# Weight decoding in a chained attention and expert kernel: GpSimd takes the signs and 26 low halves, VectorE joins a step after ScalarE's copy

## The chip, the cores and the metric

The kernel runs on one core of a Trainium2 chip. A core has a matrix engine (TensorE, PE in the profile; its weight loads are PEld), a vector engine (VectorE, DVE), a scalar engine (ScalarE, ACT), GpSimd (POOL) and SyncE (SP), which issues most of the transfers. The metric is the device time of one execution in microseconds (us), the median of several runs. Lower is better.

## The reference

Three stages follow each other, each in float32:

```python
# q, k, v: (2, 6016, 256)
qn = q / (norm(q, axis=1) + 1e-6); kn = k / (norm(k, axis=1) + 1e-6)
a = softmax(kn.transpose(0, 2, 1) @ qn / tau)           # (2, 256, 256)
x = (v @ a).reshape(12032, 256)
h = x @ w_in                                            # (12032, 2048)
x = (h - tanh(h)) @ w_out                               # (12032, 256)
return (sigmoid(x @ w_gate) * (x @ w_val)) @ w_out2     # 1536 hidden columns
```

The weights `w_in`, `w_out`, `w_gate`, `w_val` and `w_out2` arrive as float64, so each of their elements is two 32-bit words. They are the operands that this change is about.

## The kernel before, in words

**Blocks and steps.** The 12032 tokens are cut into 24 blocks of 496 or 512 columns (`blocks`, 12 for each of the two batches). The attention matrix of a batch is multiplied into `w_in` once (`aw_chunk`), so that a block needs only `H` = (A w_in) v (`emit_H`, L332 and L334), the activation (`emit_E`, L342 to L350), the product with `w_out` (`emit_X`, L373 in block 0, L378 to L381 later), and then gate, value and output (`emit_GV`, `emit_S`, `emit_O`). One turn of the main loop is a step `T`: it issues H of one of the 16 hidden tiles f of a block, the activation of the tile before it, X of the one before that, and what `gv_at` puts there of the gate stage. Block 0 has the steps 0 to 15, block 1 the steps 16 to 31. The program is written in the order in which each engine runs it: every engine, and SP's queue of transfers, takes its instructions strictly in that order and waits for semaphores where an operand is not there.

**Nearly float32 products.** Most matrix products split each operand into a rounded high half and a low half (operand minus high half) and add three products. The high half is a ScalarE copy, the low half a subtraction on VectorE.

**Weights on the way in.** `conv` turns a piece of float64 weights into float32. There are 34 pieces of 512 KB: 8 of `w_in` (`conv_win`), 8 of `w_out` (`conv_w1`), 18 of the gate stage (`conv_m2`). For each piece: a transfer into a staging tile `st` (L125); ScalarE scales the high words into `cb` (L135) and writes an f16 of them beside the mantissa bits (L136); VectorE shifts 16-bit halves (L138) and joins (L143). A piece of the gate stage then gets its high half on ScalarE (L149) and its low half on VectorE (L150). For `w_out` the halves come later, in `split_w1` (L184, L187).

**What sets the order.** `conv` is a generator. Wrapped in `whole`, it runs from one bare `yield` to the next in one step (`yield 1` does not end a step there). `at(T, ...)` starts it: its transfer is issued at the end of step T, the rest at the end of the following steps, after the activation of that step in the order of ScalarE and VectorE. The pieces of `w_out` with i > 1 start at step 2i - 1, those of the gate stage where the loop over `n` puts them.

**Buffers.** The staging tiles of `w_out` and of the gate stage come from the pool `v4`, which has 3 buffers and also holds the `v` tiles. From step 4 to step 16 one of the three holds `v` of block 1. The pieces of `w_out` then follow each other in one buffer, those of the gate stage in the other. A transfer into a buffer waits until the last reader of the piece before it is done.

Of the kernel before, what the change touches and what calls it, by code (L numbers as in the profile page):

```python
# [8 lines left out]
F32 = mybir.dt.float32  # L9
F32R = mybir.dt.float32r  # L10
BF16 = mybir.dt.bfloat16
U32 = mybir.dt.uint32
U16 = mybir.dt.uint16
F16 = mybir.dt.float16
AF = mybir.ActivationFunctionType
ALU = mybir.AluOpType
AX = mybir.AxisListType
# [10 lines left out]
def kernel(  # L28
# [13 lines left out]
    nc = tc.nc  # L42
# [18 lines left out]
    rest, i = N - WB * nb, nb // 2  # L61
    assert 0 <= rest <= nb * (TB - WB)
    while rest:
        widths[i] += QB
        rest -= QB
        i = (i + 1) % nb
    blocks = []
    for b in range(B):
        t = 0
# [23 lines left out]
    def cv(name, shape=(P, 512)):  # L93
        return cv_p.tile(list(shape), F32, tag="cv", name=name)
# [22 lines left out]
    w1_hi = [wp.tile([P, 2, C], F32R, name=f"w1h{i}") for i in range(N1 // 2)]  # L117
    w1_lo = {}
    win_d = dr_p.tile([N1 // 2, P, NK, 2 * P], F32, name="win_d")

    def conv(src, shape, pool, tag, name, w=None, hi=None, lo=None):

        a, m = shape
        st = pool.tile([P, a, 2 * m], U32, tag=tag, name=f"st_{name}")
        nc.sync.dma_start(out=st, in_=src)  # L125
        yield
        words = st.rearrange("p a (m t) -> p a m t", t=2)
        low, high = words[:, :, :, 0], words[:, :, :, 1]
        half = st.bitcast(U16).rearrange("p a (m t) -> p a m t", t=4)
        bt = cv(f"cb_{name}", (P, a, m))  # L130
        bu = bt.bitcast(U32)

        nc.scalar.activation(bt, high.bitcast(F32), AF.Copy, scale=2.0**-112)  # L135
        nc.scalar.activation(half[:, :, :, 3].bitcast(F16), high.bitcast(F32), AF.Copy, scale=2.0**-96)  # L136
        yield 1
        nc.vector.tensor_scalar(half[:, :, :, 2], half[:, :, :, 1], 13, None, ALU.logical_shift_right)  # L138
        yield 1
        yield 1  # L140
        if callable(w):
            w = w()
        nc.vector.scalar_tensor_tensor(  # L143
            out=bu if w is None else w.bitcast(U32), in0=bu, scalar=3, in1=high,
            op0=ALU.logical_shift_left, op1=ALU.bitwise_or
        )
        if w is None:
            yield
            nc.scalar.activation(hi, bt, AF.Copy)  # L149
            nc.vector.tensor_tensor(out=lo, in0=bt, in1=hi.bitcast(F32), op=ALU.subtract)  # L150

    def whole(g):

        for x in g:
            if x is None:
                yield

    def words(ap):
        return ap.bitcast(U32)

    def conv_win(i, pool, tag="st"):
        src = words(w_in)[:, i * 512:(i + 1) * 512].rearrange("(k p) f -> p k f", p=P)
        yield from conv(src, (NK, 2 * P), pool, tag, f"wi{i}", w=win[i])
# [7 lines left out]
    w1_f = {}  # L171

    def conv_w1(i):
        src = words(w_out)[i * 256:(i + 1) * 256, :].rearrange("(a p) d -> p a d", p=P)

        def home():
            pool, tag = (wp, f"w1l{i - 4}") if i > 3 else (wp2, f"w2{'hl'[i % 2]}{4 + i // 2}")
            w1_f[i] = pool.tile([P, 2, C], F32, tag=tag, name=f"w1f{i}")
            return w1_f[i]

        return conv(src, (2, C), v4_p, "v4", f"w1{i}", w=home)

    def split_w1(i):
        nc.scalar.activation(w1_hi[i], w1_f[i], AF.Copy)  # L184
        yield
        w1_lo[i] = wp.tile([P, 2, C], F32R, tag=f"w1l{i}", name=f"w1l{i}")
        nc.vector.tensor_tensor(out=w1_lo[i], in0=w1_f[i], in1=w1_hi[i].bitcast(F32), op=ALU.subtract)  # L187


    kq = {}  # L190
# [291 lines left out]
    while len(e_of) < NT:  # L482
        for home in ("x2h", "x2l", *(f"rr{i}" for i in range(6))):
            j = len(e_of)
            n = min(2 if home[0] == "x" else 1, NT - j)
# [174 lines left out]
    def conv_m2(i, which):  # L660
        if which == 2:
            src = words(w_out2)[i * 256:(i + 1) * 256, :].rearrange("(a p) d -> p a d", p=P)
            for x, nm in ((w2_hi, "w2h"), (w2_lo, "w2l")):
                x[i] = wp2.tile([P, 2, 2 * P], F32R, tag=f"{nm}{i}", name=f"{nm}{i}")
            h, lo = w2_hi[i], w2_lo[i]
        else:
            w = (w_gate, w_val)[which]
            src = words(w)[:, i * 512:(i + 1) * 512].rearrange("(k p) f -> p k f", p=P)
            h, lo = ((wg_hi[i], wg_lo[i]), (wv_hi[i], wv_lo[i]))[which]
        return conv(src, (2, 2 * P), v4_p, "v4", f"m{which}{i}", hi=h, lo=lo)  # L670
# [31 lines left out]
    def at(step, fn, *a):  # L702
        bg.setdefault(step, []).append((fn, a))
# [3 lines left out]
    GV0 = (20, 21, 22, 24, 25, 27, 28, 30, 31, 33, 34, 35)  # L707
# [6 lines left out]
    for i in range(N1 // 2):  # L714
        at({6: 16, 2: 18, 7: 19, 3: 20, 4: 21, 5: 23, 0: 25, 1: 26}[i], split_w1, i)
# [4 lines left out]
            at(2 * i - 9 if i < 6 else 2 * i - 5, win_store, i)  # L720
    for n in range(3 * N2 // 2):
        i, w = divmod(n, 3)
        late = GV0[2 * i] - 3 + (w == 2)
        at(min(late, 4 + 2 * n if n < 6 else 7 + 3 * n // 2), lambda i=i, w=w: whole(conv_m2(i, w)))
    at(2 * N1 + 7, ks_load)
    for j in range(NT):
        t = 54 + 2 * j
# [121 lines left out]
```

## Time and profile before

| | us |
|---|---|
| median of 3 runs | 2211.52 (2211.27 to 2211.89) |
| profiled execution, its own time | 2212.01 |
| its span in the profile | 2210.2 |
| TensorE busy | 2199.5 |
| VectorE busy | 1772.7 |
| ScalarE busy | 1602.0 |
| GpSimd busy | 66.5 |

The span runs from the first to the last instruction of the program; the execution's own time has 1.8 us around it. A matmul's recorded time overlaps with the next one's, so a busy TensorE says that it had work, not how fast it went. The granted clock of TensorE is 1.00 in all slices. GpSimd's 46 additions (L688) lie between 366 and 858 us, and all 34 pieces of weights between 2 and 246 us.

### The profile page before, as it was taken

What the parts mean: (1) busy time and instruction counts of PE and PEld (TensorE: products, weight loads), DVE (VectorE), ACT (ScalarE), POOL (GpSimd) and SP (SyncE); (2) the same over time, 40 slices, a digit from 0 to 9 for tenths busy, and PEclk for the clock granted to TensorE, in tenths of its full rate; (3) what the DMA queues carried; (4) which work ended last, traced back from release to release, by engine and by line L of the source; (5) the groups of instructions that cost most, each with busy time, mean ns of one, the idle gap of its engine ahead of it and who ended that gap; (6) DMA issues with size and microseconds to landing.
All of it is one profiled execution on the core that took longest, in us unless ns stands there. A gap on an engine that the chain in (4) does not pass through costs nothing.

```text
span 2210.2 us, 28820 instructions
## 1 busy us (share of the span) xinstructions
PE 2199.5 (100%) x10338; PEld 1944.1 (88%) x10338; DVE 1772.7 (80%) x2723; ACT 1602.0 (72%) x2811; POOL 66.5 (3%) x53
## 2 busy tenths in 40 slices
PE   9999999999999999999999999999999999999999
PEld 8778899898888888888999999999988888888898
DVE  7889877888888888878787787787787877877773
ACT  7988867777777777767677676776776776767763
POOL 0000000111111110000000000000000000000000
PEclk9999999999999999999999999999999999999999
DMA  9742101111111010001000000000000000000000
GB/s 354 241 147 96 38 1 53 34 29 52 35 29 48 27 36 20 1 24 34 19 19 1 19 19 1 19 19 1 19 20 1 19 20 1 20 1 19 10 1 19
DMA packets 54000, 86.54 MB, mean 39 GB/s; under 512 B 4960, under 2 KB 31072, under 8 KB 53856
## 3 DMA queue, kind: packets, MB, share of 16 engines
q1 hardware_dynamic: 53280, 83.91, 11.6%
q8 instruction: 81, 1.33, 0.3%
q10 hardware_dynamic: 576, 0.79, 0.1%
q14 instruction: 63, 0.52, 0.1%
HBM read 69.73 MB, written 14.94 MB: 38 GB/s over the span
## 4 chain that ended last, share of the span: by engine, by line
PE 93%; DVE 3%; ACT 3%; issue 1%; DMA 1%; ACTq 0%; DVEq 0%
PE o L445 16%; PE h L332 14%; PE h L334 7%; PE x L381 7%; PE x L378 7%; PE x L379 7%; PE va L414 5%; PE va L416 5%; PE va L413 5%; PE ga L414 5%; PE ga L413 5%; PE ga L416 5%; PE x L373 2%; PE kqe L517 1%; PE aw L285 1%
## 5 line engine op out<-in xcount | busy, mean ns | idle before, releaser
L347 DVE SCALAR_TENSOR_TENSOR w<-u,h 128x496 f32<-128x496 f32 (+1 forms) x384 | 259.6, 676 | 228.6 <-ACT t L343 227.7
L350 DVE COPY_PREDICATED w<-m,t 128x496 f32<-128x496 uint16 (+1 forms) x384 | 303.9, 792 | 39.9 <-ACT sr L687 0.5
L342 ACT ACTIVATE u<-h 128x496 f32<-128x496 f32 (+1 forms) x384 | 222.7, 580 | 138.8 <-PE h L334 138.3
L345 ACT ACTIVATE s<-u,cb 128x496 f32<-128x496 f32 (+1 forms) x384 | 273.8, 713 | 0.3 <-DVE w L349 0.3
L346 ACT ACTIVATE m<-u,ct 128x496 bf16<-128x496 f32 (+1 forms) x384 | 272.5, 710 | 0.0
L348 DVE TENSOR_TENSOR t<-h,t 128x496 f32<-128x496 f32 (+1 forms) x384 | 258.4, 673 | 0.0
L349 DVE SCALAR_TENSOR_TENSOR w<-s,w 128x496 f32<-128x496 f32 (+1 forms) x384 | 257.6, 671 | 0.0
L332 PE MATMUL h<-vTh,awh 128*128 128x496 f32 (+1 forms) x768 | 232.8, 385 | 0.0
L334 PE MATMUL h<-vTh,awl 128*128 128x496 f32 (+1 forms) x768 | 225.1, 375 | 0.2 <-DVE awl L291 0.2
L332 PE MATMUL h<-vTl,awh 128*128 128x496 f32 (+1 forms) x768 | 225.0, 375 | 0.0
L343 ACT ACTIVATE t<-h 128x496 f32<-128x496 f32 (+1 forms) x384 | 223.1, 581 | 0.0
L414 PE MATMUL va<-x2h,wvl 128*128 128x496 f32 (+1 forms) x552 | 206.9, 375 | 0.0
L414 PE MATMUL ga<-x2h,wgl 128*128 128x496 f32 (+1 forms) x552 | 206.9, 375 | 0.0
L413 PE MATMUL va<-x2h,wvh 128*128 128x496 f32 (+1 forms) x552 | 206.9, 375 | 0.0
L413 PE MATMUL ga<-x2h,wgh 128*128 128x496 f32 (+1 forms) x552 | 206.8, 375 | 0.0
L425 DVE TENSOR_TENSOR sg<-va,sg 128x496 f32<-128x496 f32 (+1 forms) x288 | 192.2, 667 | 18.1 <-PE va L416 18.1
L424 ACT ACTIVATE sg<-ga 128x496 f32<-128x496 f32 (+1 forms) x288 | 168.6, 585 | 11.2 <-PE ga L416 11.1
L416 PE MATMUL ga<-x2l,wgh 128*128 128x496 f32 (+1 forms) x576 | 168.8, 375 | 0.0
L416 PE MATMUL va<-x2l,wvh 128*128 128x496 f32 (+1 forms) x576 | 168.8, 375 | 0.0
L332 PEld LDWEIGHTS h<-vTh,awh 128*128 128x128 f32 x768 | 144.4, 189 | 24.5 <-issue 6.8
L334 PEld LDWEIGHTS h<-vTh,awl 128*128 128x128 f32 x768 | 145.1, 189 | 17.7 <-DVE awl L291 0.6
L332 PEld LDWEIGHTS h<-vTl,awh 128*128 128x128 f32 x768 | 145.1, 189 | 17.2
(358 smaller groups left out, 4425.8 us busy)
## 6 DMA issues: line engine op xcount, KB each, us to landing
v<-in_v_dram SPq DMA_DIRECT2D x16, 496.0 KB, 4.2
out_dram<-ob SPq DMA_DIRECT2D x15, 496.0 KB, 3.0
sr<-in_q_dram SPq DMA_DIRECT2D x47, 128.0 KB, 2.1
sr<-in_k_dram SPq DMA_DIRECT2D x47, 128.0 KB, 2.3
raw<-in_q_dram SPq DMA_DIRECT2D x13, 384.0 KB, 8.1
raw<-in_k_dram SPq DMA_DIRECT2D x12, 384.0 KB, 8.2
st_wi<-in_moe_w_in_dram SPq DMA_DIRECT2D x8, 512.0 KB, 7.0
st_w<-in_moe_w_out_dram SPq DMA_DIRECT2D x8, 512.0 KB, 4.7
```

The lines of the kernel that those rows point to most:

```text
L332: MM(o[:, :n], aw_hi[i][:, kk, fs], turned(p, x[:, kk, :n]), start=x is h and kk == 0, stop=False)
L334: MM(o[:, :n], aw_lo[i][:, kk, fs], turned(p, h[:, kk, :n]), start=False, stop=kk == 1)
L345: nc.scalar.activation(s, u, AF.Square, bias=cb)
L346: nc.scalar.activation(m, u, AF.Relu, bias=ct2)
L347: nc.vector.scalar_tensor_tensor(out=w, in0=u, scalar=C2, in1=hp, op0=ALU.mult, op1=ALU.mult)
L348: nc.vector.tensor_tensor(out=t, in0=hp, in1=t, op=ALU.subtract)
L349: nc.vector.scalar_tensor_tensor(out=w, in0=s, scalar=CG, in1=w, op0=ALU.add, op1=ALU.mult)
L350: nc.vector.copy_predicated(w, m.bitcast(U16), t)
L413: MM(o[:, :n], wht[m // 2][:, d, ms], h[d], start=d == 0, stop=False)
L414: MM(o[:, :n], wlt[m // 2][:, d, ms], h[d], start=False, stop=False)
L416: MM(o[:, :n], wht[m // 2][:, d, ms], lo[d], start=False, stop=d == 1)
L445: MM(ops[p][d][:, :n], w[i][:, a, ds[d]], x, start=m == 0 and w is w2_hi and x is ph, stop=m == N2 - 1 and x is pl)
```

## The change

`conv` no longer writes the f16 on ScalarE (L136) and no longer shifts halves on VectorE (L138). GpSimd instead overwrites the high words with their sign bits, in the same step as ScalarE's copy and after it. A step later VectorE shifts the low words by 29 and joins the signs to them, in place, and then joins the result with the copy. The bare `yield` between GpSimd and VectorE is the step. The subtraction for the low half moves to GpSimd for the 18 pieces of the gate stage and for the 8 of `split_w1`. The pieces of the gate stage start one step earlier; those of `w_out` start where they did.

```diff
--- before.py
+++ after.py
@@ -11,7 +11,7 @@
 BF16 = mybir.dt.bfloat16
 U32 = mybir.dt.uint32
 U16 = mybir.dt.uint16
-F16 = mybir.dt.float16
+I32 = mybir.dt.int32
 AF = mybir.ActivationFunctionType
 ALU = mybir.AluOpType
 AX = mybir.AxisListType
@@ -126,28 +126,28 @@
         yield
         words = st.rearrange("p a (m t) -> p a m t", t=2)
         low, high = words[:, :, :, 0], words[:, :, :, 1]
-        half = st.bitcast(U16).rearrange("p a (m t) -> p a m t", t=4)
         bt = cv(f"cb_{name}", (P, a, m))
         bu = bt.bitcast(U32)
 
 
-
         nc.scalar.activation(bt, high.bitcast(F32), AF.Copy, scale=2.0**-112)
-        nc.scalar.activation(half[:, :, :, 3].bitcast(F16), high.bitcast(F32), AF.Copy, scale=2.0**-96)
+        nc.gpsimd.tensor_scalar(high.bitcast(I32), high.bitcast(F32), 0.0, -2.0**31, ALU.is_lt, ALU.mult)
         yield 1
-        nc.vector.tensor_scalar(half[:, :, :, 2], half[:, :, :, 1], 13, None, ALU.logical_shift_right)
-        yield 1
+        yield
+        nc.vector.scalar_tensor_tensor(
+            out=low, in0=low, scalar=29, in1=high, op0=ALU.logical_shift_right, op1=ALU.bitwise_or
+        )
         yield 1
         if callable(w):
             w = w()
         nc.vector.scalar_tensor_tensor(
-            out=bu if w is None else w.bitcast(U32), in0=bu, scalar=3, in1=high,
+            out=bu if w is None else w.bitcast(U32), in0=bu, scalar=3, in1=low,
             op0=ALU.logical_shift_left, op1=ALU.bitwise_or
         )
         if w is None:
             yield
             nc.scalar.activation(hi, bt, AF.Copy)
-            nc.vector.tensor_tensor(out=lo, in0=bt, in1=hi.bitcast(F32), op=ALU.subtract)
+            nc.gpsimd.tensor_tensor(out=lo, in0=bt, in1=hi.bitcast(F32), op=ALU.subtract)
 
     def whole(g):
 
@@ -184,7 +184,7 @@
         nc.scalar.activation(w1_hi[i], w1_f[i], AF.Copy)
         yield
         w1_lo[i] = wp.tile([P, 2, C], F32R, tag=f"w1l{i}", name=f"w1l{i}")
-        nc.vector.tensor_tensor(out=w1_lo[i], in0=w1_f[i], in1=w1_hi[i].bitcast(F32), op=ALU.subtract)
+        nc.gpsimd.tensor_tensor(out=w1_lo[i], in0=w1_f[i], in1=w1_hi[i].bitcast(F32), op=ALU.subtract)
 
 
     kq = {}
@@ -720,8 +720,8 @@
             at(2 * i - 9 if i < 6 else 2 * i - 5, win_store, i)
     for n in range(3 * N2 // 2):
         i, w = divmod(n, 3)
-        late = GV0[2 * i] - 3 + (w == 2)
-        at(min(late, 4 + 2 * n if n < 6 else 7 + 3 * n // 2), lambda i=i, w=w: whole(conv_m2(i, w)))
+        late = GV0[2 * i] - 4 + (w == 2)
+        at(min(late, 3 + 2 * n if n < 6 else 6 + 3 * n // 2), lambda i=i, w=w: whole(conv_m2(i, w)))
     at(2 * N1 + 7, ks_load)
     for j in range(NT):
         t = 54 + 2 * j
```

The order of SP's queue at steps 5 and 7 (`st_w13` is piece 3 of `w_out`, `st_m10` the first `w_val` piece, `er` are tiles of q and k). Before:

```order
L125 DMA st_w13_780<-in_moe_w_out_dram 128x2x512
L502 DMA er18_821<-in_q_dram 128x256
L502 DMA er18_821<-in_k_dram 128x256
L125 DMA st_m10_824<-in_moe2_w_val_dram 128x2x512
```

After:

```order
L125 DMA st_w13_780<-in_moe_w_out_dram 128x2x512
L125 DMA st_m10_782<-in_moe2_w_val_dram 128x2x512
L502 DMA er18_823<-in_q_dram 128x256
L502 DMA er18_823<-in_k_dram 128x256
L502 DMA er19_858<-in_q_dram 128x256
L502 DMA er19_858<-in_k_dram 128x256
L502 DMA er20_861<-in_q_dram 128x256
L502 DMA er20_861<-in_k_dram 128x256
L125 DMA st_w14_864<-in_moe_w_out_dram 128x2x512
L166 DMA win_d_124<-win6_114 128x512
L125 DMA st_m20_869<-in_moe2_w_out_dram 128x2x512
```

The two pieces that were issued a step apart are issued together, at the odd step, and the next two at the next odd step.

ScalarE at step 10 (`u`, `t`, `s`, `m` are the activation of tile 9, `cb` the copies out of the staging tiles). Before:

```order
L342 ACTIVATE u_9_954<-h_9_929 128x496
L343 ACTIVATE t_9_955<-h_9_929 128x496
L345 ACTIVATE s_9_956<-u_9_954,cb 128x496
L346 ACTIVATE m_9_958<-u_9_954,ct 128x496
L149 ACTIVATE w2h_909<-cb_m_940 128x512
L135 ACTIVATE cb_w_987<-st_w_951 128x512
L136 ACTIVATE st_w_951<-st_w_951 128x512
```

After:

```order
L342 ACTIVATE u_9_956<-h_9_929 128x496
L343 ACTIVATE t_9_957<-h_9_929 128x496
L345 ACTIVATE s_9_958<-u_9_956,cb 128x496
L346 ACTIVATE m_9_960<-u_9_956,ct 128x496
L149 ACTIVATE w2h_867<-cb_m_907 128x512
L133 ACTIVATE cb_w_989<-st_w_951 128x512
L133 ACTIVATE cb_m_992<-st_m_954 128x512
L342 ACTIVATE u_10_995<-h_10_969 128x496
```

One copy and one f16 write have become two copies, both ahead of the activation of tile 10 in step 11.

VectorE at step 9 (`w` closes the activation of tile 8, `awl` is the low half of a part of A w_in, `w1f` a decoded piece of `w_out`). Before:

```order
L350 COPY_PREDICATED w_8_916<-m_8_917,t_8_914 128x496
L291 TENSOR_TENSOR awl_926<-aw_5_887,awh_105 128x512
L138 TENSOR_SCALAR st_m_911<-st_m_911 128x512
L143 SCALAR_TENSOR_TENSOR cb_m_940<-cb_m_940,st_m_911 128x512
```

After:

```order
L350 COPY_PREDICATED w_8_916<-m_8_917,t_8_914 128x496
L291 TENSOR_TENSOR awl_926<-aw_5_891,awh_105 128x512
L137 SCALAR_TENSOR_TENSOR st_w_864<-st_w_864 128x512
L143 SCALAR_TENSOR_TENSOR w1f_941<-cb_w_904,st_w_864 128x512
L137 SCALAR_TENSOR_TENSOR st_m_869<-st_m_869 128x512
L143 SCALAR_TENSOR_TENSOR cb_m_907<-cb_m_907,st_m_869 128x512
```

Two pieces are joined here, both copied in step 8, and they are the last instructions of the odd step; in the even step nothing is joined.

## Rows read from the trace of the kernel before

**Rows 1.** The page, part 1: busy us (share of the span) x instructions, by engine.
```profile
PE 2199.5 (100%) x10338; PEld 1944.1 (88%) x10338; DVE 1772.7 (80%) x2723; ACT 1602.0 (72%) x2811; POOL 66.5 (3%) x53
```

**Rows 2.** Waits of TensorE, whole run: total us, times, longest us.
```profile
PE va L414 <- DVE wvl L150: 1.5, 1, 1.5
PE x L378 <- ACT g_14h L355: 0.6, 1, 0.6
PE rq L236 <- DVE dg L223: 0.5, 1, 0.5
PE ep L267 <- DVE s L257: 0.5, 2, 0.4
PE h L334 <- DVE awl L291: 0.2, 1, 0.2
```

**Rows 3.** Windows: stretch, length, then busy us (x instructions) of each engine, clock, DMA.
```profile
100.00:110.00 10.00, 10.00 (x41) 7.46 (x40) 8.79 (x15) 9.02 (x15) 0.00 (x0) 1.00 0.66 189
220.00:240.00 20.00, 18.22 (x83) 14.87 (x81) 19.30 (x31) 18.30 (x31) 0.00 (x0) 1.00 0.12 41
```

**Rows 4.** Groups by line, 0 to 420 us: shape, xcount | busy us, mean ns | idle.
```profile
L136 ACT ACTIVATE st_m<-st_m 128x512 f16<-128x512 f32 x18 | 24.5, 1363 | 0.6
L138 DVE TENSOR_SCALAR st_m<-st_m 128x512 uint16<-128x512 uint16 x18 | 13.5, 748 | 2.4 <-ACT st_m L136 2.4
L135 ACT ACTIVATE cb_m<-st_m 128x512 f32<-128x512 f32 x18 | 12.1, 674 | 0.0
L150 DVE TENSOR_TENSOR w2l<-cb_m,w2h 128x512 fp32r<-128x512 f32 x6 | 4.1, 682 | 0.0
```

**Rows 5.** DMA issues: KB each, median us from issue to landing.
```profile
st_w<-in_moe_w_out_dram SPq DMA_DIRECT2D x8, 512.0 KB, 4.7
st_m<-in_moe_w_val_dram SPq DMA_DIRECT2D x6, 512.0 KB, 4.6
```

**Rows 6.** Waits of the SP queue, whole run: total us, times, longest us.
```profile
SPq L125 <- DVE cb_m L143: 19.8, 6, 6.6
```

**Rows 7.** Timeline of ScalarE, steps 10 to 12: start us, us, instruction [idle <-releaser].
```profile
105.05 0.58 ACT L342 ACTIVATE u<-h 128x496 f32<-128x496 f32 x1 [0.92 <-PE h L334]
107.72 0.67 ACT L135 ACTIVATE cb_w<-st_w 128x512 f32<-128x512 f32 x1
115.20 0.58 ACT L342 ACTIVATE u<-h 128x496 f32<-128x496 f32 x1 [0.91 <-PE h L334]
```

**Rows 8.** Timeline of VectorE, steps 5, 6 and 10.
```profile
83.63 0.74 DVE L350 COPY_PREDICATED w<-m,t 128x496 f32<-128x496 uint16 x1
84.24 0.69 DVE L291 TENSOR_TENSOR awl<-aw,awh 128x512 fp32r<-128x512 f32 x1
84.86 0.74 DVE L138 TENSOR_SCALAR st_m<-st_m 128x512 uint16<-128x512 uint16 x1
85.64 0.69 DVE L143 SCALAR_TENSOR_TENSOR cb_m<-cb_m,st_m 128x512 uint32<-128x512 uint32 x1
86.25 0.66 DVE L347 SCALAR_TENSOR_TENSOR w<-u,h 128x496 f32<-128x496 f32 x1
108.08 0.73 DVE L350 COPY_PREDICATED w<-m,t 128x496 f32<-128x496 uint16 x1
```

**Rows 9.** Timeline of TensorE, steps 14 and 16.
```profile
128.52 0.58 PE L334 MATMUL h<-vTh,awl 128*128 128x496 f32 x2
137.83 1.83 PE L373 MATMUL x<-w,w1f 128*128 128x496 f32 x4
```

**Rows 10.** Timeline of GpSimd and VectorE at 377 us.
```profile
377.65 1.27 POOL L688 TENSOR_TENSOR acc<-acc,sr 128x512 f32<-128x512 f32 x1 [10.26 <-ACT sr L687]
377.78 1.72 DVE L350 COPY_PREDICATED w<-m,t 128x496 f32<-128x496 uint16 x1
```

**Rows 11.** Timelines of ScalarE and VectorE ahead of the longest wait.
```profile
237.32 0.64 ACT L149 ACTIVATE wvh<-cb_m 128x512 fp32r<-128x512 f32 x1
239.54 0.68 DVE L150 TENSOR_TENSOR wvl<-cb_m,wvh 128x512 fp32r<-128x512 f32 x1
```

## The prediction

> **What bounds the kernel now.** I read the busy table first, then TensorE's waits, then windows, then timelines of single steps. TensorE is busy for 2199.5 of 2210.2 us [rows 1]. Its waits for a computed operand are few: 1.5 us for a low half of a `w_val` piece, 0.6 for `g_14h`, 0.5 and 0.5 in the first softmax, 0.2 for `awl` [rows 2], 3.3 us in all. So nothing that relieves ScalarE or VectorE can give back more than about 3.3 us, 0.15%; a measurement of this kernel can tell about 0.2%, 4.4 us, from no change. A loss has no such limit. The helpers run close behind TensorE: in steps 9 and 10 ScalarE is busy 9.02 and VectorE 8.79 of 10 us, and at 220 to 240 us VectorE 19.30 and ScalarE 18.30 of 20 [rows 3].
>
> **What goes.** Every piece loses the f16 write, 1.36 us of ScalarE, and a 0.75 us shift on VectorE [rows 4], in place of which VectorE gets a second shift-and-or like L143, 0.69 us [rows 8]. ScalarE so loses 34 x 1.36 = 46 us. 26 low halves of 0.68 us [rows 4] leave VectorE, 18 us. Of all this TensorE feels at most the 3.3 us above. I take 1.5 of it: the longest wait ends with VectorE's low half at 239.54 + 0.68 = 240.22; its high half ended at 237.32 + 0.64 = 237.96 [rows 11], so GpSimd, at 1.27 us for such an operation [rows 10], can end it by 239.2, 1.0 us earlier; and half of the 1.0 us in the softmax, where one f16 write stands ahead of the chain. Bounds: nothing to 3.3.
>
> **What GpSimd costs.** The sign operation is not in the trace. Its nearest rows are GpSimd's two-operand add of the same 128x512, 1.27 us [rows 10], and ScalarE's copy of the same strided words, 0.67 us [rows 4]; I take the slower, since it is the same engine, and keep 0.67 to 2.5 (twice the add). The engine has room: 34 x 1.27 + 26 x 1.27 = 76 us over 240. A price on VectorE is shown: with GpSimd's add beginning at 377.65, VectorE's `w<-m,t` took 1.72 us [rows 10] against 0.73 when alone [rows 8], so an operation of GpSimd can hold up VectorE by 1.0 us. A low half that cost VectorE 0.68 us costs it 0 to 1.0 now, as it meets such an instruction or not; a sign the same or less. I take the 26 low halves as even and the signs as hidden, and keep up to 3 us for both.
>
> The Trainium skill (SBUF — State Buffer, section "Who interferes with whom") speaks against the change here: a VectorE instruction with two SBUF inputs and a GpSimd instruction that reads SBUF exclude each other, and the later one blocks fully. By it the wait would be the rest of the add, 377.65 + 1.27 - 377.78 = 1.14 us, where the row shows 1.0; the trace agrees in kind, and the sum would be the same.
>
> **What is moved: the loop through the staging buffers.** This is the term that decides. From step 5 on, two pieces are issued at an odd step right after the joins of the two pieces before them, into the same two buffers; their copies stand in ScalarE's order at the end of the even step, ahead of the activation of the next odd step; their joins stand in VectorE's order behind that activation; and the next transfers wait for those joins. So there is a closed loop of two steps, in which nothing overlaps:
> - transfer, issue to landing: 4.6 us [rows 5];
> - ScalarE's copy of the second piece: 0.67 [rows 7];
> - from the first instruction of the activation (105.05) to VectorE's last one (108.08): 3.03 [rows 7, 8];
> - from there past `awl` to the first join: 84.86 - 83.63 = 1.23 [rows 8];
> - two pairs of VectorE instructions, from their starts: 0.78 + 0.61 + 0.78, and the last one's 0.69: 2.86 [rows 8].
>
> That is 12.39 us a loop. TensorE's own two steps take 115.20 - 105.05 = 10.15 us, both starts released by its H [rows 7]. The loop is 2.24 us too long, so the activation falls behind by that much every two steps. Before, the two pieces alternate between the steps, and the copy of one, and its join, come in the step after the transfer; the queue waits for joins there as well (19.8 us in 6 waits [rows 6]), without a wait on TensorE behind it.
>
> How far behind, counted out. The first pair of joins, in step 5, follows `w<-m,t` at 83.63: 83.63 + 1.23 + 2.86 = 87.72. Transfer and copy: 87.72 + 4.6 + 0.67 = 92.99, the activation's start in step 7. Four loops on, in step 15, it starts at 92.99 + 4 x 12.39 = 142.55. The last piece of `w_out` is joined there (no `awl` in that step) 3.03 + 0.61 + 0.78 + 0.69 = 5.11 later, at 147.66. Its matmuls, X of tile 14, began at 137.83 [rows 9]: 9.8 us late. The low half `awl` of step 13 is late first: 142.55 - 12.39 = 130.16, plus 3.03 + 0.61 + 0.69, is 134.49, against 128.52 [rows 9], 6.0 us. These two are the same delay seen twice, not a sum. What hides the beginning is the lead that activation and joins have over H and X, some 4 to 5 us; it is used up after the second loop.
>
> Its bounds: transfer and handoffs may differ by 0.6 us a loop, over four loops 2.4 either way; two transfers at once are the slower case. And up to 1.5 us more can follow at step 16, where a copy waits once more. The signs hide in the loop: from the copy's end to the join there are 3.03 + 1.23 = 4.26 us, room for two signs of 1.27, and for two of 2.1.
>
> **The sum.** +9.8 for the loop, -1.5 for what is relieved, 0 for GpSimd: +8.3 us on the profiled execution's own 2212.0, that is 2220.3; the median of the runs lies 0.5 below that execution, so 2219.8. With its bounds, 2215.5 to 2226.
>
> **Rivals.**
> 1. The loop does not bind. If the copies are in time (a transfer that lands in 2.4 us instead of 4.6 would do it: 12.39 - 2.24 = 10.15), ScalarE's wait is only idle time and what is left is the relief less what GpSimd disturbs: 2211.5 - 1.5 = 2210.0, within 2208.2 to 2215. For it: ScalarE loses 1.36 us a piece, and idles 0.92 us behind H even now [rows 7]. Against it: that slack can't shorten a chain of waits.
> 2. The faster side: relief alone, at the places of [rows 2]. If every one of the five waits goes, and the shorter ScalarE queue also closes gaps that the profile doesn't name as waits (a tenth of a microsecond here and there, 1 to 2 us), the time is 2211.5 - 3.3 - 1.5 = 2206.7. It decides only if the loop is shorter than 10.15 us and VectorE loses nothing at 220 to 240.
> 3. GpSimd against VectorE. At 200 to 245 us, where VectorE has 19.30 of 20 us taken [rows 3], five low halves leave (5 x 0.68 = 3.4 us) and five low halves and four signs come, at up to 1.0 us each [rows 10]: 9.0. VectorE would then be 5.6 us over, and what TensorE waits there grows by that: without the loop 2211.5 + 5.6 - 1.0 = 2216.1, with it some 2225. This is what the Trainium skill's rule on the shared port, cited above (SBUF — State Buffer), would make of the change if every operation met one of VectorE's. For it: the block in [rows 10]. Against it: half of VectorE's instructions read PSUM and one SBUF tile.
>
> **Chances.** The loop is a count over instructions whose order and durations are known, so 0.66 for the forecast. Rival 1 0.22, rival 2 0.04, rival 3 without the loop 0.08 (half of it slower by over 0.2%). Faster by over 0.2% (below 2207.1): 0.04. Slower (above 2215.9): 0.64 of the forecast's 0.66, and 0.04: 0.68. Same: 0.28. The range for 8 in 10 leaves out the faster rival and the low end of rival 1, about 1 in 10, and as much above: 2209 to 2226.
>
> **What would show it.** Right: in the profile after, ScalarE waits for `st_w` and `st_m` transfers in steps 6 to 14, 2 to 4 us each time; the activations of the odd steps are 12 to 13 us apart between 90 and 145 us; TensorE waits for `awl` or for X's weights between 105 and 150 us, 7 to 12 us in all; the wait for `wvl` shrinks from 1.5 us to under 1. Wrong: steps of 10.1 us in block 0 (rival 1), or waits of TensorE that lie at 200 to 245 us with VectorE's instructions stretched to 1.2 us or more (rival 3). A sign that takes over 2.1 us would lengthen the loop further.

## The result, and the profile after

The changed kernel took 2224.52 us (median of 4 runs, 2223.99 to 2225.79) against 2211.70 for the kernel before in the same comparison (2211.27 to 2212.30): a ratio of 1.0059, 95% interval 1.0041 to 1.0076, slower by 12.8 us. The forecast was 2219.8, range 2209 to 2226. The profiled execution took 2225.01 us with a span of 2223.2. Page, part 1, of the changed kernel (beside [rows 1]):

```profile
PE 2201.9 (99%) x10338; PEld 1944.0 (87%) x10338; DVE 1774.8 (80%) x2697; ACT 1560.7 (70%) x2777; POOL 181.2 (8%) x113
```

ScalarE has 41 us less work than before and GpSimd 115 us more. VectorE has 2 us more: the first join takes what the shift took, and the 18 us of low halves that left it came back as longer instructions. TensorE is recorded as busy for 2.4 us more; the span grew by 13.0. The rest is waits. Waits of TensorE, whole run: total us, times, longest us (beside [rows 2]).

```profile
PE h L332 <- ACT awh L290: 3.6, 3, 2.1
PE x L373 <- DVE w1f L143: 3.1, 1, 3.1
PE h L334 <- DVE awl L291: 2.8, 4, 1.3
PE x L378 <- ACT g_14h L355: 1.4, 1, 1.4
PE x L378 <- ACT g_11h L355: 1.1, 1, 1.1
...
PE va L414 <- POOL wvl L150: 0.8, 1, 0.8
```

The wait for `wvl` shrank from 1.5 to 0.8, as forecast; the waits for `awh`, `w1f` and `awl` are new or longer, and they lie in block 0. Timeline of TensorE, four of the eleven instructions between 57 and 245 us with a wait of 0.3 us or more ahead of them (start us, us, instruction [idle <-releaser]); the last is the row that answers to [rows 9].

```profile
62.91 0.69 PE L334 MATMUL h<-vTh,awl 128*128 128x496 f32 x2 [1.35 <-DVE awl L291]
...
108.59 0.69 PE L332 MATMUL h<-vTh,awh 128*128 128x496 f32 x2 [0.54 <-ACT awh L290]
...
134.01 0.69 PE L332 MATMUL h<-vTh,awh 128*128 128x496 f32 x2 [2.09 <-ACT awh L290]
...
148.41 1.93 PE L373 MATMUL x<-w,w1f 128*128 128x496 f32 x4 [3.14 <-DVE w1f L143]
```

Both traces hold the same 10338 matmuls in the same order, so each can be set against itself. The delay of the changed kernel, by the places where it jumps by more than 0.3 us:

| place (time in the kernel before) | jump, us |
|---|---|
| start, up to 13 us | -0.5 |
| `awl` of the first step, 62 | +1.0 |
| `awh` and `awl` of steps 10, 12, 14 (H), 107 to 129 | +6.6 |
| X of tile 14, 138 | +3.5 |
| three places at 140 to 152 | +1.3 |
| `g_11h`, 212 | +1.35 |
| `g_14h`, 228 | +0.9 |
| behind `g_14h` up to `wvl`, 229 to 240 | -0.95, of which -0.7 at `wvl` |
| 439 | -0.4 |
| last matmul | +12.8 |

So 10.1 us come between 107 and 138 us, in block 0, and the rest from smaller places of both signs. The -0.5 at the start I don't count as an effect of the change: it arises at waits for the first transfers of q and k, and over the profiles of the ten kernels below it lies between -0.7 and +0.1, whichever engine has the work. The 1.3 at 140 to 152 are three jumps of 0.35, 0.35 and 0.6 that I didn't trace to one cause. The prediction had kept up to 1.5 us for a copy that waits once more at step 16; nothing arises there in e8 and e10 below, which have neither the loop nor work on GpSimd, and 1.7 in e9, which has the loop alone.

**The loop.** Timelines of ScalarE, VectorE and SP, steps 9 to 11: one turn of the loop through the staging buffers (beside [rows 7, 8]).

```profile
105.25 0.67 ACT L133 ACTIVATE cb_m<-st_m 128x512 f32<-128x512 f32 x1 [1.46 <-DMA st_m<-in_moe_w_out_dram]
...
105.83 0.56 ACT L342 ACTIVATE u<-h 128x496 f32<-128x496 f32 x1
...
108.83 0.73 DVE L350 COPY_PREDICATED w<-m,t 128x496 f32<-128x496 uint16 x1
...
109.45 0.68 DVE L291 TENSOR_TENSOR awl<-aw,awh 128x512 fp32r<-128x512 f32 x1
...
110.04 0.68 DVE L137 SCALAR_TENSOR_TENSOR st_w<-st_w 128x512 uint32<-128x512 uint32 x1
...
112.09 0.69 DVE L143 SCALAR_TENSOR_TENSOR cb_m<-cb_m,st_m 128x512 uint32<-128x512 uint32 x1
...
112.84 0.38 SPq L125 DMA_DIRECT2D st_m<-in_moe_w_gate_dram  x1
```

And ScalarE at the end of the turn, the same view:

```profile
117.41 0.67 ACT L133 ACTIVATE cb_m<-st_m 128x512 f32<-128x512 f32 x1 [1.24 <-DMA st_m<-in_moe_w_gate_dram]
117.98 0.56 ACT L342 ACTIVATE u<-h 128x496 f32<-128x496 f32 x1
```

From the copy of the second piece (105.25) the activation of tile 8 follows at 105.83; its last VectorE instruction at 108.83; `awl` and the first join at 110.04; the last join ends at 112.09 + 0.69 = 112.78 and releases the transfer at 112.84; the copy that waits for it begins at 117.41, 4.57 us later, and the activation of tile 10 at 117.98. That is 12.15 us, in which nothing overlaps. The first and the last of the five activations that stand in this place (tiles 6, 8, 10, 12, 14), timeline of ScalarE:

```profile
93.42 0.56 ACT L342 ACTIVATE u<-h 128x496 f32<-128x496 f32 x1
...
143.34 0.57 ACT L342 ACTIVATE u<-h 128x496 f32<-128x496 f32 x1
```

The waits of the SP queue from 80 to 150 us that answer to [rows 6]; most of them now end with the join of a `w_out` piece, the first of a pair:

```profile
SPq L125 <- DVE w1f L143: 43.1, 6, 10.4
```

In the same stretch before, the queue waited 15.1 us for joins, in 5 waits; the 19.8 us of [rows 6], which the prediction put into block 0, are of the whole run. ScalarE waits for staging transfers in that stretch of the changed kernel, 17.5 us in all and 1.2 to 2.7 at a time (forecast: 2 to 4); before, it had no such wait there. Four turns took 143.34 - 93.42 = 49.9 us, 12.48 each, where the kernel before took 10.1.

**GpSimd.** Groups by line of the changed kernel, 0 to 420 us (beside [rows 4]): shape, xcount | busy us, mean ns | idle.

```profile
L134 POOL TENSOR_SCALAR st_m<-st_m 128x512 int32<-128x512 f32 x18 | 40.2, 2235 | 13.8 <-ACT cb_m L133 11.3 <-issue 1.6 <-POOL w1l L187 0.7
...
L137 DVE SCALAR_TENSOR_TENSOR st_m<-st_m 128x512 uint32<-128x512 uint32 x18 | 14.3, 795 | 0.0
...
L187 POOL TENSOR_TENSOR w1l<-w1f,w1h 128x512 fp32r<-128x512 f32 x8 | 12.9, 1607 | 0.0
...
L150 POOL TENSOR_TENSOR w2l<-cb_m,w2h 128x512 fp32r<-128x512 f32 x6 | 8.8, 1459 | 22.7 <-ACT w2h L149 19.6 <-issue 3.1
```

A sign takes GpSimd 2.24 us (2.10 to 2.47 in the groups of the other pieces), not the 1.27 that I took. Timelines of GpSimd and VectorE ahead of the wait for `g_11h` (beside [rows 10]):

```profile
221.07 0.66 DVE L348 TENSOR_TENSOR t<-h,t 128x496 f32<-128x496 f32 x1
...
221.25 1.27 POOL L150 TENSOR_TENSOR wvl<-cb_m,wvh 128x512 fp32r<-128x512 f32 x1 [2.41 <-ACT wvh L149]
...
221.65 1.41 DVE L349 SCALAR_TENSOR_TENSOR w<-s,w 128x496 f32<-128x496 f32 x1
...
222.50 2.41 POOL L134 TENSOR_SCALAR st_m<-st_m 128x512 int32<-128x512 f32 x1
...
223.16 0.96 DVE L350 COPY_PREDICATED w<-m,t 128x496 f32<-128x496 uint16 x1
```

L349 has both inputs in SBUF and takes 0.66 us alone; it begins 0.40 after GpSimd's low half and ends 0.54 after it: 0.75 us lost. L348 ahead of it reads PSUM and isn't touched. L350 loses 0.24 to the sign behind. And in the window of 220 to 240 us (beside [rows 3]) VectorE is as full as it was, though the low halves have left it (the work in the window has moved by 12 to 14 us):

```profile
220.00:240.00 20.00, 18.93 (x89) 16.47 (x88) 19.22 (x27) 14.71 (x27) 9.03 (x6) 1.00 0.32 92
```

Timelines of GpSimd and VectorE before the first step, where the delay of 1.0 us at 62 arises:

```profile
58.33 3.93 POOL L134 TENSOR_SCALAR st_w<-st_w 128x512 int32<-128x512 f32 x2 [6.13 <-ACT cb_w L133]
...
60.36 1.10 DVE L137 SCALAR_TENSOR_TENSOR st_w<-st_w 128x512 uint32<-128x512 uint32 x1 [2.32 <-POOL st_w L134]
...
62.17 0.68 DVE L291 TENSOR_TENSOR awl<-aw,awh 128x512 fp32r<-128x512 f32 x1
```

The first row is two signs in a row, 3.93 us. VectorE waits 2.32 us for the first of them, joins that piece (the first join takes 1.10 us beside the second sign, 0.68 alone), and `awl`, which TensorE waits for, stands behind. Before, VectorE waited there 2.35 us for the f16 write; without that write it now waits as long for the sign. The row of the kernel before:

```profile
60.26 0.75 DVE L138 TENSOR_SCALAR st_w<-st_w 128x512 uint16<-128x512 uint16 x1 [2.35 <-ACT st_w L136]
```

### The profile page after: what moved, and what is told of

The parts are those of the page before. It is cut to its first block, busy times and chain, and to the rows that moved or that the text cites. A ratio compares the mean times of both kernels' runs of the same rounds, so it can differ in the third digit from the quotient of the medians.

```text
span 2223.2 us, 28896 instructions
## 1 busy us (share of the span) xinstructions
PE 2201.9 (99%) x10338; PEld 1944.0 (87%) x10338; DVE 1774.8 (80%) x2697; ACT 1560.7 (70%) x2777; POOL 181.2 (8%) x113
## 4 chain that ended last, share of the span: by engine, by line
PE 87%; DVE 5%; DMA 3%; ACT 3%; issue 2%; POOL 0%; SPq 0%; ACTq 0%; DVEq 0%; POOLq 0%
PE o L445 16%; PE h L332 13%; PE x L381 7%; PE h L334 7%; PE x L378 6%; PE x L379 6%; PE va L414 5%; PE va L416 5%; PE va L413 5%; PE ga L416 5%; PE ga L414 5%; PE ga L413 5%; DMA raw<-in_k_dram 1%; DVE w L349 1%; DVE w L350 1%
## 5 line engine op out<-in xcount | busy, mean ns | idle before, releaser
L347 DVE SCALAR_TENSOR_TENSOR w<-u,h 128x496 f32<-128x496 f32 (+1 forms) x384 | 259.3, 675 | 244.6 <-ACT t L343 243.9
L350 DVE COPY_PREDICATED w<-m,t 128x496 f32<-128x496 uint16 (+1 forms) x384 | 306.4, 798 | 40.9 <-DVE w L349 0.9
L349 DVE SCALAR_TENSOR_TENSOR w<-s,w 128x496 f32<-128x496 f32 (+1 forms) x384 | 266.3, 693 | 0.0
L348 DVE TENSOR_TENSOR t<-h,t 128x496 f32<-128x496 f32 (+1 forms) x384 | 258.1, 672 | 0.0
L425 DVE TENSOR_TENSOR sg<-va,sg 128x496 f32<-128x496 f32 (+1 forms) x288 | 191.8, 666 | 18.1 <-PE va L416 18.1
```

What stands on the lines that cost most here:

```text
L347: nc.vector.scalar_tensor_tensor(out=w, in0=u, scalar=C2, in1=hp, op0=ALU.mult, op1=ALU.mult)
L348: nc.vector.tensor_tensor(out=t, in0=hp, in1=t, op=ALU.subtract)
L349: nc.vector.scalar_tensor_tensor(out=w, in0=s, scalar=CG, in1=w, op0=ALU.add, op1=ALU.mult)
L350: nc.vector.copy_predicated(w, m.bitcast(U16), t)
```

## The experiments

Ten kernels, against two theories. **The loop:** two pieces per two steps, transfer, copy, activation and joins in a chain of 12.15 us against TensorE's 10.15. **GpSimd:** its instructions hold up VectorE's, and that is what slows block 0. The cadence is from the start of the activation of tile 6 to that of tile 14, over four; the last column is how much later X of tile 14 begins than the 137.83 of the kernel before.

| kernel | time, us | before, us | ratio (95%) | cadence | X of tile 14 |
|---|---|---|---|---|---|
| changed kernel | 2224.52 | 2211.70 | 1.0059 (1.0041 to 1.0076) | 12.48 | +10.6 |
| e1, stagger | 2217.66 | 2211.64 | 1.0028 (1.0017 to 1.0040) | 10.70 | +1.9 |
| e2, v late | 2215.90 | 2211.64 | 1.0020 (1.0011 to 1.0029) | 10.69 | +1.3 |
| e3, no GpSimd | 2222.39 | 2211.64 | 1.0048 (1.0036 to 1.0061) | 12.19 | +8.5 |
| e4, same step | 2239.17 | 2211.64 | 1.0123 (1.0110 to 1.0137) | 10.73 | +11.8 |
| e5, v late, no GpSimd | 2211.50 | 2211.83 | 0.9999 (0.9990 to 1.0008) | 10.41 | -0.1 |
| e6, v late, signs only | 2215.45 | 2211.83 | 1.0018 (1.0009 to 1.0027) | 10.65 | +0.6 |
| e7, low halves only | 2216.21 | 2211.83 | 1.0020 (1.0011 to 1.0029) | 10.10 | -0.2 |
| e8, sign on VectorE | 2211.43 | 2211.83 | 0.9998 (0.9990 to 1.0007) | 10.11 | -1.4 |
| e9, later join alone | 2230.54 | 2211.58 | 1.0088 (1.0074 to 1.0102) | 13.96 | +17.9 |
| e10, e8 and earlier | 2212.53 | 2211.58 | 1.0004 (0.9995 to 1.0013) | 10.07 | -1.0 |

**e1: the pieces of a pair a step apart again.**

```diff
-        at(min(late, 3 + 2 * n if n < 6 else 6 + 3 * n // 2), ...
+        at(min(late, 4 + 2 * n if n < 6 else 6 + 3 * n // 2), ...
```

> The change, but the first six pieces of the gate stage start where they did before the change (steps 4, 6, 8, 10, 12, 14 instead of 3 to 13), so that the two pieces of a pair are again a step apart. GpSimd keeps all 34 signs and 26 low halves, VectorE still joins a step late. Theory (the two-step loop through the staging buffers costs 10.1 us in block 0): each piece has a loop of its own, with one join and a transfer that has the engines to itself, 3.03 + 1.21 + 0.72 + 0.69 + 0.3 + 3.6 + 0.58 = 10.1 us, no longer than TensorE's 10.15, so ScalarE's waits for staging transfers in steps 6 to 15 fall from 15 us to under 5, X of tile 14 begins within 2 us of where it did before the change (137.8), and the time is 2213 to 2217. Rival (GpSimd's hold on VectorE's operands slows the activations of block 0): as many GpSimd instructions meet as many activations, so X of tile 14 stays at 146 to 149 and the time at 2222 to 2226.

Timeline of ScalarE in e1, activations of tiles 6 and 14:

```profile
90.39 0.56 ACT L342 ACTIVATE u<-h 128x496 f32<-128x496 f32 x1
...
133.21 0.57 ACT L342 ACTIVATE u<-h 128x496 f32<-128x496 f32 x1
```

The largest of ScalarE's waits in e1 from 80 to 150 us (total us, times, longest us):

```profile
ACT cb_w L133 <- DMA st_w<-in_moe_w_out_dram: 15.3, 5, 3.9
```

The cadence falls to 10.70 and X of tile 14 begins at 139.69. The loop of each piece still is 0.6 us longer than TensorE's two steps. GpSimd stretches both joins of a `w_out` piece in each of the four turns, L137 to 1.16 us (0.68 without) and L143 to 1.03 (0.69 without), 0.8 us together, which is enough for it; e1 without GpSimd was not run. One of those rows, of step 9 (timeline of VectorE):

```profile
105.67 1.16 DVE L137 SCALAR_TENSOR_TENSOR st_w<-st_w 128x512 uint32<-128x512 uint32 x1
```

The time, 2217.66, is 0.7 above the range that the loop theory gave and 4.3 us below the rival's. Another expectation missed by more: ScalarE's waits for transfers were to fall under 5 us and came to 20.4, more than the 17.5 of the changed kernel. They cost little here (X of tile 14 is 1.9 us late, 0.9 of it from 62 us): a wait is no loss by itself; the cadence is what tells.

**e2: the third buffer takes part.**

```diff
-        if e0 and e0[1] == (4 if T < N1 else 12) and e0[0] + 1 < NB:
+        if e0 and e0[1] == 12 and e0[0] + 1 < NB:
```

> The change, but v of block 1 is loaded at step 12 instead of step 4, so that the third buffer of the pool takes part in the staging until step 12. Theory (staging loop): at each odd step only the first piece of a pair still waits for a join, and for the first join instead of the second, so the loop loses 1.33 us and some 0.6 us of a shared transfer, 12.15 - 1.9 = 10.2 us; the slip of 2.0 us a loop becomes 0 to 0.6 us until step 11 and comes back for one or two loops behind it. X of tile 14 at 139 to 143, the time 2214 to 2219. Rival (GpSimd's hold on VectorE): nothing moves, 2222 to 2226.

Timeline of ScalarE in e2, activations of tiles 6 and 14:

```profile
91.31 0.57 ACT L342 ACTIVATE u<-h 128x496 f32<-128x496 f32 x1
...
134.06 0.57 ACT L342 ACTIVATE u<-h 128x496 f32<-128x496 f32 x1
```

Four turns of 10.91, 10.18, 10.18 and 11.48 (the last one after the buffer is taken by `v`), X of tile 14 at 139.14, 2215.90 us: as the loop theory said, with every sign and low half still on GpSimd.

**e3: GpSimd left out.**

```diff
-        nc.gpsimd.tensor_scalar(high.bitcast(I32), ...
+        nc.vector.tensor_scalar(high.bitcast(I32), ...
-            nc.gpsimd.tensor_tensor(out=lo, ...
+            nc.vector.tensor_tensor(out=lo, ...
-        nc.gpsimd.tensor_tensor(out=w1_lo[i], ...
+        nc.vector.tensor_tensor(out=w1_lo[i], ...
```

> The change with every instruction that it gave to GpSimd put on VectorE in the same place of the program: 34 signs, 26 low halves. Joins, starts and buffers stay. Theory (staging loop): the loop's terms have no GpSimd in them; VectorE's sign stands behind ScalarE's copy and ahead of the next activation, where VectorE waits anyway, so X of tile 14 is again 9 to 13 us late (147 to 151), and the time is 2221 to 2227. The waits for g_11h and g_14h of 1.1 and 1.4 us at 212 to 242 may be any size, since VectorE has 0.7 us a piece more to do there. Rival (GpSimd's hold on VectorE makes the loss): no instruction of GpSimd is left before 366 us, the time falls to 2211 to 2214.

Timeline of ScalarE in e3, activations of tiles 6 and 14:

```profile
92.52 0.56 ACT L342 ACTIVATE u<-h 128x496 f32<-128x496 f32 x1
...
141.29 0.57 ACT L342 ACTIVATE u<-h 128x496 f32<-128x496 f32 x1
```

The sign on VectorE in e3 (groups by line, 0 to 400 us; xcount | busy us, mean ns | idle):

```profile
L134 DVE TENSOR_SCALAR st_m<-st_m 128x512 int32<-128x512 f32 x18 | 7.7, 425 | 8.6 <-ACT cb_m L133 8.6
```

No sign and no low half is on GpSimd, and the loop is still there, 12.19 us a turn. X of tile 14 begins at 146.38, 0.6 earlier than I had given; the time, 2222.39, is in the range of the loop theory and 8 us above the rival's. What went are the losses at 62 and 212 to 228 us. And the sign costs VectorE 0.43 us, a fifth of what it costs GpSimd.

**e4: joins in the step of the copy.**

```diff
         yield 1
-        yield
+        yield 1
         nc.vector.scalar_tensor_tensor(
```

> The change without the bare yield between GpSimd's sign and VectorE's joins: VectorE joins in the step of ScalarE's copy, as before the change, and waits there for the sign. GpSimd keeps everything. Theory (staging loop): the buffers come free a step earlier, so no transfer waits on the loop, and ScalarE's waits for transfers in steps 6 to 15 vanish; in its place VectorE waits for two signs of 2.0 us at each odd step, about 2 x 2.1 + 0.7 - 1.5 = 3.4 us, which the lead of the activation over X (4 to 5 us) can cover, so 2212 to 2218. Rival (GpSimd's hold on VectorE): no gain, 2222 to 2226, or more through the waits for the signs.

Waits of VectorE in e4, whole run (total us, times, longest us), the largest group that ends with a sign, and then the two largest of TensorE:

```profile
DVE st_m L137 <- POOL st_m L134: 16.6, 10, 4.4
```

```profile
PE x L373 <- DVE w L350: 4.8, 2, 3.9
PE n L203 <- DVE accb L585: 4.5, 1, 4.5
```

The cadence is 10.73, so the loop of 12.15 us is gone. But the time is 2239.17, far above what either theory gave. I had priced the signs' wait in block 0 alone, where TensorE's delay grows by 3.4 us. It grows by 8.4 before that (VectorE's squares stand behind the signs, and TensorE waits 4.5 us for `accb`) and by 16 in the steps behind, where VectorE has no slack. So the bare yield is not a free choice: with a sign of 2 us on GpSimd, leaving it out made the changed kernel 14.7 us slower.

**e5: both edits, e2's and e3's.**

> Both of the edits that worked on different losses: v of block 1 loaded at step 12, and all 34 signs and 26 low halves on VectorE. If the two losses are separate (staging loop in block 0; GpSimd holding up VectorE at 62, 212 and 228 us), they add: TensorE's delay against the kernel before is -0.6 us at 62 us, as with no GpSimd alone, +1.6 more in block 0, as with the late v alone, +0.5 at 212, -0.5 at 439, in sum +1.0, so 2212.7, within 2211 to 2214.5. If GpSimd's instructions were part of the loop, or VectorE's added work became the bound once the loop is gone, it stays above 2215.

2211.50 us: they add up, a little better than given. Loop and GpSimd together are the whole loss, within the 2 us that the interval leaves. Between e2 and e5 lie 4.4 us, all that GpSimd costs with the loop out of the way.

**e6: e2 with the low halves on VectorE**, the signs alone on GpSimd.

> v of block 1 loaded at step 12, the 26 low halves back on VectorE, the 34 signs on GpSimd. Theory (a low half on GpSimd holds up VectorE's L349 and L350 at 212 and 228 us and shortens the wait for wvl; the sign does so at 62 us): the two losses of 1.3 and 0.9 us and the gain of 0.9 us go, 2215.9 - 2.2 + 0.9 = 2214.6, within 2213.5 to 2215.5. Rival (the signs are what holds VectorE up there, 2.0 to 2.5 us each): no less than 2215.5, the waits for g_11h and g_14h stay.

Waits of TensorE in e6:

```profile
PE va L414 <- DVE wvl L150: 1.5, 1, 1.5
...
PE x L378 <- ACT g_14h L355: 0.5, 1, 0.5
```

The wait for `g_11h` has left the list, that for `g_14h` is back at 0.5 and that for `wvl` at 1.5, as without the change: those three belong to the low halves. The wait for `awl` at 62 us stays, 1.3 us: it belongs to the sign. The median, 2215.45, is at the edge of the theory's range, only 0.45 us below e2's. In the profiled execution 1.3 us of TensorE's delay arise at 503 us, where no sign and no low half runs. There one of GpSimd's 46 additions, which the kernel before has too, meets VectorE (timelines of GpSimd and VectorE in e6):

```profile
497.23 1.27 POOL L688 TENSOR_TENSOR acc<-acc,sr 128x512 f32<-128x512 f32 x1 [10.24 <-ACT sr L687]
...
497.40 1.68 DVE L350 COPY_PREDICATED w<-m,t 128x496 f32<-128x496 uint16 x1 [0.45 <-ACT sr L687]
```

In e2 the same addition began 0.19 us behind that L350, which took 0.72 us, and nothing arises at 503. So by these rows 1.0 of the 1.3 us goes back to such a meeting, not to the signs; it was not tried, and how often it comes in the other executions of e6, which lie between 2214.7 and 2217.8, isn't known.

**e7: the kernel before, with the 26 low halves on GpSimd and nothing else.**

> The kernel before with nothing but the 26 low halves moved to GpSimd. No loop, no signs, joins in the same step. Theory: +1.3 and +0.9 us at 212 and 228, -0.9 at the wait for wvl, up to 0.6 at 152: +1.3 to 1.9 us, 2212.5 to 2214. Rival (the low halves cost nothing, the signs make those waits): 2210.5 to 2212.

Timeline of VectorE in e7, ahead of the waits for `g_11h` and `g_14h`:

```profile
211.11 1.41 DVE L349 SCALAR_TENSOR_TENSOR w<-s,w 128x496 f32<-128x496 f32 x1
...
229.37 1.59 DVE L350 COPY_PREDICATED w<-m,t 128x496 f32<-128x496 uint16 x1
```

Slower by 4.4 us, more than twice what I gave. The two waits and `wvl` came as expected (+1.5, +0.9, -0.85); four smaller ones of 0.4 to 0.7 us at 195, 209, 224 and 242 us came with them. Why they came here and not in the changed kernel isn't shown. The prices of signs and low halves don't add up: by the medians, the signs alone make 3.95 us (e5 to e6), the low halves on top of them 0.45 (e6 to e2), and the low halves alone 4.4 here.

**e8: the sign on VectorE, joined in the same step, the starts of before, nothing on GpSimd.**

```diff
-        nc.gpsimd.tensor_scalar(high.bitcast(I32), ...
+        nc.vector.tensor_scalar(high.bitcast(I32), ...
         yield 1
-        yield
+        yield 1
...
-        late = GV0[2 * i] - 4 + (w == 2)
-        at(min(late, 3 + 2 * n if n < 6 else 6 + 3 * n // 2), ...
+        late = GV0[2 * i] - 3 + (w == 2)
+        at(min(late, 4 + 2 * n if n < 6 else 7 + 3 * n // 2), ...
```

(and both low halves on VectorE, as in e3)

> A version that may beat both: no f16 write on ScalarE and no shift, as in the change, but the sign on VectorE (0.43 us there), the joins in the step of ScalarE's copy, the starts of before, nothing on GpSimd. VectorE has 0.43 + 0.69 us a piece instead of 0.75, ScalarE 1.36 less. Expected: -0.6 us at 62 us, where the f16 write stood ahead of the join, nothing in block 0, 0 to +1.5 at 212 to 240, where VectorE has 19.3 of 20 us taken: 2210 to 2213. If VectorE's 0.37 us more a piece is what binds there, more than 2213.

2211.43 against 2211.83: within what I gave, and no difference that can be told. In the profiled execution TensorE is 1.3 us ahead of the kernel before at 62 us and 0.6 ahead at the end.

**e9: the kernel before, with the change's order alone.**

```diff
         nc.scalar.activation(half[:, :, :, 3].bitcast(F16), ...
         yield 1
+        yield
         nc.vector.tensor_scalar(half[:, :, :, 2], half[:, :, :, 1], 13, ...
         yield 1
-        yield 1
...
-        late = GV0[2 * i] - 3 + (w == 2)
-        at(min(late, 4 + 2 * n if n < 6 else 7 + 3 * n // 2), ...
+        late = GV0[2 * i] - 4 + (w == 2)
+        at(min(late, 3 + 2 * n if n < 6 else 6 + 3 * n // 2), ...
```

> The kernel before, f16 write on ScalarE and shift on VectorE and nothing on GpSimd, with the order of the change alone: shift and join one step behind ScalarE, the gate stage's pieces started one step earlier. Theory (staging loop): the loop is the same as the change's with ScalarE's f16 write of the second piece in it, 12.15 + 1.36 + 0.1 = 13.6 us against TensorE's 10.15, a slip of 3.45 us a loop instead of 2.0. The activation of step 7 and the four loops behind it are 5 x 1.4 = 7 us later than in the changed kernel; X of tile 14, 10.1 us late there without the softmax's 0.5, is 15 to 19 us late, and the time is 2225 to 2231. Rival (the loss hangs on GpSimd or on what the joins and signs do, not on when they stand): 2211 to 2214.

Timeline of ScalarE in e9, activations of tiles 6 and 14, and one of the f16 writes that stand in the loop:

```profile
94.69 0.66 ACT L342 ACTIVATE u<-h 128x496 f32<-128x496 f32 x1
...
122.29 1.35 ACT L136 ACTIVATE st_m<-st_m 128x512 f16<-128x512 f32 x1
...
150.53 0.67 ACT L342 ACTIVATE u<-h 128x496 f32<-128x496 f32 x1
```

The strongest evidence for the loop: GpSimd has nothing to do, the arithmetic is the old one, and the cadence is 13.96, longer than the changed kernel's by 1.48, where the f16 write in it takes 1.35. X of tile 14 is 17.9 us late, the time 2230.54, both within what was given. The order has two changes, the later join and the earlier starts of the gate stage's pieces. In the changed kernel e4 takes back the first alone and e1 the second alone, and either brings the cadence to 10.7: the loop needs both.

**e10: e8 with the last twelve pieces a step earlier.**

> The version with the sign on VectorE, joins in the same step and nothing on GpSimd, with the last twelve pieces of the gate stage started one step earlier, as in the change. Expected: the wait of 1.5 us for wvl at 240 us goes, since that piece is decoded a step earlier; nothing else moves more than 0.5 us: 2209.5 to 2211.0. Rival (VectorE's queue at 200 to 240 us has no room for it, and the waits come back at another tile): 2211 to 2213.

The rival was right: the wait for `wvl` went (-1.6 us at 240), and waits of 1.7 and 0.6 us for `g_14l` and `g_15l` came ahead of it. The time, 2212.53, is in its range, and no different from the kernel before. VectorE has no room there; the piece can be decoded late or the activations can be late.

## Why the prediction was right, and where it was off

**The loop: right, and nearly to size.** Forecast was 12.39 us a turn and an activation of step 15 at 142.55; the turns took 12.11 to 13.25, 12.48 on average, and the activation began at 143.34. Of the terms, in the turn shown, the transfer with its handoff took 4.57 for 4.6, the copy to the activation 0.58 for 0.67, the activation 3.00 for 3.03, `awl` 1.21 for 1.23, the joins 2.74 for 2.86, and 0.06 to the next issue, for which I had no term. In the one turn of 13.25 the copy stood 5.65 us behind the issue. X of tile 14 was 10.6 us late for a forecast 9.8, of which 0.5 were there from 62 us on. The low half of step 13 was 7.1 late for 6.0. One place was not named: ScalarE's `awh` stands behind the same activation and was waited for as well, 3.6 us. Those waits are the same delay seen earlier. e1 and e2 took most of the loop's slip away and left GpSimd, e3 took GpSimd away and left the loop, e9 made the loop without GpSimd: that it makes the 10 us is shown.

**"-1.5 for what is relieved": half right.** `wvl` gave 0.7 of the forecast 1.0 (its wait fell from 1.46 to 0.77). The softmax gave nothing of its 0.5: its two waits are 0.7 and 0.4 us, in sum 1.1 for 1.0 before, and 0.4 in e3, without GpSimd; in the changed kernel a subtraction of VectorE ahead of them (L311) took 1.63 us beside a sign, 1.19 alone. And behind the softmax, at the `awl` of 62 us, 1.0 was lost, for which the sum had no term: the step said that an f16 write goes, and left out that the sign comes in its place. With a sign of 0.43 us on VectorE (e3) TensorE is 0.6 us ahead of the kernel before at 62 us, where the changed kernel is 0.5 behind it.

**"0 for GpSimd": the term that was wrong.** I took the 26 low halves as even and the signs as hidden, up to 3 us for both. Two sizes were off. A sign takes 2.1 to 2.5 us, near the upper end of the range that I had kept (2.5) and not the 1.27 that I took; in the loop it was hidden all the same (12.48 us a turn, 12.19 without GpSimd in e3). And the low halves aren't even: alone they make 4.4 us in e7, and with the signs 4.4 from e5 to e2. In the changed kernel, where the loop's delay gave some of it cover, GpSimd costs 2224.52 - 2222.39 = 2.1 us. So rival 3 was not wrong: what was to show it, VectorE's instructions stretched to 1.2 us or more and waits of TensorE between 200 and 245 us, came beside what was to show the loop. It was smaller than its 5.6 us, 2.25 at `g_11h` and `g_14h` less what `wvl` gave, and that its "some 2225" with the loop lies at the measured 2224.52 is luck. The Trainium skill (GPSIMD Engine Reference, section "Engine selection") puts GpSimd at about twice VectorE's time for two-operand work and calls one-operand work roughly line-rate: for the subtraction, 1.27 us when nothing meets it against 0.68 agrees with the first; for the sign, 2.24 against 0.43 does not agree with the second. The sum by what was measured: +10.1 for the loop, +1.0 and -0.5 ahead of it, +1.3 at 140 to 152, +2.25 - 0.95 at 212 to 240, -0.4 at 439, 12.8.

The Trainium skill (SBUF — State Buffer, section "Who interferes with whom") has it that a VectorE instruction with two SBUF inputs contends with a GpSimd instruction that reads SBUF, for a shared port that it calls an exclusive lock; of VectorE's two-port modes it says that the later one fully blocks. For the low half the trace agrees with a full block: L349, begun at 221.65, ends 0.54 us after the low half that began ahead of it, its own length less 0.12. For the sign it does not hold to the end of the instruction: the L350 that began at 223.16, 1.75 us before the end of a sign, lost 0.24 us.

**Rival 1** (the loop does not bind) fell: it needed a transfer of 2.4 us, and in those steps no copy began less than 3.2 us after its transfer's issue. **Rival 2** needed a loop shorter than 10.15 us and nothing lost on VectorE; neither was so. The range held, because its upper end was set by the loop with GpSimd's price.

## What to carry to other kernels

Before work is moved a step later, count the buffer that it holds: from the join through transfer, copy and the work that stands between in the in-order queues back to the join. If that sum is longer than the steps for which the buffers last, every turn slips, and the helpers look idle meanwhile (at 100 to 110 us ScalarE was busy for 6.06 of 10 us, 9.02 before). Relief of an engine that bounds nothing gives nothing back (41 us of ScalarE here, and 2211.43 for 2211.83 in e8); an operation that goes to GpSimd is to be priced by what it takes there (here 2.2 us for 0.43) and by the VectorE instructions with two SBUF operands that it meets. Where VectorE was busy for 19 of 20 us, moving a piece earlier moved the wait and didn't end it (e10).

## What the runs showed of the hardware

- The same sign instruction on the same 128x512 words: 2.1 to 2.5 us on GpSimd by the means of its three groups, 3.93 for two in a row, 0.43 us on VectorE. The subtraction: 1.27 us on GpSimd when nothing meets it, 1.34 to 1.61 by the means of its groups, against 0.68.
- Which VectorE instructions GpSimd holds up, from 60 to 400 us of the changed kernel, worked out from the rows that overlap one of GpSimd's: L347, L348 and L425, which read PSUM, never over 0.68 us in 46 meetings. L349, with both inputs in SBUF, takes 0.66 us alone and 1.36 on average in 12 meetings with a low half of the gate stage, up to 1.65; those that began in the first 0.4 us of the low half all ended 0.53 or 0.54 us behind it.
- A sign holds VectorE up in its first part only. L350, whose mask and data lie in SBUF, takes 0.72 us alone; the 8 that met a sign alone and began in the first 0.8 us of a sign took 0.74 to 1.16 and ended 0.77 to 0.80 us before that sign did. L349 kept its 0.66 us in 10 meetings with a sign alone; one of them began together with the sign, and none of the others in its first 0.8 us. The joins (L143), also with both inputs in SBUF, kept their 0.69 us in 8 that began over 1.2 us into a sign, took 1.03 in the 4 of e1 that began 0.6 us into one, and 1.65 in 3 with a low half of `split_w1`. Why the low half holds VectorE to its end and the sign doesn't was not tried.
